# Linear attention feeding an RWKV channel mix: q transposed on TensorE instead of by DMA, units of 512/384/256 tokens with attention paced evenly, later loads on the GpSimd queue

## The chip, the cores and the metric

One core of one Trainium2 chip. The metric is device time in microseconds (us) of one execution, as a median of several. A ratio is the mean time of one kernel's fast runs over that of the other's in the same rounds, so it is not quite the ratio of the medians quoted beside it.

## The reference, cut to what matters

```python
# q, k, v: [8 batches, 8 heads, 576 tokens, 64], float32
q_s = softmax(q, over the 64 features);  k_s = softmax(k, over the 576 tokens)
kv  = einsum('bhsd,bhse->bhde', k_s, v)
x   = einsum('bhsd,bhde->bhse', q_s, kv)          # then heads side by side: [8, 576, 512]
xk, xr = x mixed with the token before it, by mu_k and by mu_r
k   = relu(xk @ w_k)                              # 512 -> 1024
out = sigmoid(xr @ w_r) * ((k * k) @ w_v)         # 1024 -> 512
```

## The kernel before

Attention runs in groups: 4 heads of one batch, 16 groups in all. A group loads q, k and v (0.59 MB each), takes exponentials on ScalarE, and TensorE forms `kv` (`kvp` in the code). To multiply the softmax of q by it, q must be transposed. The DMA engines do that:

```python
qt = apool.tile([128, J, 128], BF16, tag="qt", name="qt")
nc.sync.dma_start_transpose(out=qt[:], in_=qs[:].rearrange("p j c -> p (j c)"))
yield
for hf in range(2):
    ...                                    # cut: xp = kv^T q^T on TensorE, copied to xb by ScalarE
...                                        # cut: VectorE mixes xb with itself shifted: xd, xm, xk, xr
```

All loads, all transposes and all stores go through the SyncE queue, in that engine's order; the ten weight loads go through GpSimd's. TensorE's matmuls write to tiles of the pool `psum`, of which the channel mix has four (the PSUM buffers below). The channel mix works in 12 units of 384 tokens: 8 relu blocks of 4 matmuls into `kfp` (ScalarE takes the relu, VectorE squares it), then for each 128 tokens 4 matmuls into `rp` (ScalarE takes the tanh) and 8 into `vp` (VectorE multiplies and the result goes out). Both halves are generators and are interleaved:

```python
ASTEPS = 16            # an attention batch has 14 steps, so 16 a batch runs ahead of the units
MSTEPS = 14
for n in range(NU):                                            # NU = 12 units
    goal0 = done
    if n == 0:
        goal = ASTEPS
    else:
        goal = min((B - 1) * ASTEPS, ASTEPS + int(ASTEPS * n / 1.5) + 1)
    for i, _ in enumerate(unit(n)):
        want = goal0 + (goal - goal0) * (i + 1) // MSTEPS
        while done < want:
            next(att, None)
            done += 1
```

Below, "first unit" is the first piece of channel mix, and a "group" of batch 1 is "batch 1, group 0" or "group 1". A scheduler fixes each engine's order of instructions when the kernel is built. What stands behind a waiting instruction waits with it.

The softmax here doesn't subtract the row's maximum and nothing guards it: scores larger than these inputs give would overflow.

## Time and profile before

| | before |
|---|---|
| time, median (range) | 229.42 us (229.09 to 230.0) |
| span of the profiled run, TensorE clock granted | 228.1 us, 0.983 |
| busy: TensorE / VectorE / ScalarE | 182.5 / 160.1 / 136.0 us |
| first `vp` matmul; last matmul done | 50.3; 223.1 us |

The first `vp` matmul is a good milestone: the start is over by then, and nearly all the channel mix is still to come. The slices, stages and chain of this profile are shown in the prediction.

### The profile page before, as it was taken

Reading aid. Unit: us, or ns where it says so; the run is one execution under the profiler, and the core shown is the slowest. Engines: PE = TensorE matmul, PEld = TensorE weight load, DVE = VectorE, ACT = ScalarE, POOL = GpSimd, SP = SyncE. Lnnn points to the kernel's source line nnn. Section 1 sums busy time; section 2 is a strip of 40 time slices with the busy share of each in tenths; the row PEclk is TensorE's granted clock in tenths of the full one; section 3 lists DMA queues with packets and bytes.
Section 4 is the critical chain, followed back from the end, with each engine's and each line's share of the span. In section 5 each row is a group of like instructions: output and inputs, shape, how many; then the busy total and the mean of one; then the engine's idle time right before and its main releaser. Section 6 shows DMA issues by size and latency. Waiting matters only on the chain.

```text
span 228.1 us, 3352 instructions
## 1 busy us (share of the span) xinstructions
PE 182.5 (80%) x1153; PEld 92.8 (41%) x1169; DVE 160.1 (70%) x367; ACT 136.0 (60%) x213; POOL 7.1 (3%) x16
## 2 busy tenths in 40 slices
PE   0100055599989989979999999999999999999991
PEld 0100032254543534434544545545545454554540
DVE  0550077899989999799999999995867843343521
ACT  4544048699597886697685994946437254352720
POOL 2360000000000000000000000000000000000000
PEclk9999999599999999999999999999999999999999
DMA  6999999999799999999899899444041140414114
GB/s 222 362 318 207 195 314 393 259 334 285 171 303 295 247 318 232 279 293 275 282 264 313 248 277 275 92 93 98 3 92 46 40 101 1 111 26 95 46 46 95
DMA packets 40009, 45.32 MB, mean 199 GB/s; under 512 B 21048, under 2 KB 22584, under 8 KB 39992
## 3 DMA queue, kind: packets, MB, share of 16 engines
q1 hardware_dynamic: 37760, 42.48, 66.8%
q0 software_dynamic: 2208, 2.62, 6.7%
q8 instruction: 9, 0.15, 0.3%
q14 instruction: 8, 0.07, 0.1%
q10 hardware_dynamic: 24, 0.00, 0.0%
HBM read 33.56 MB, written 9.44 MB: 189 GB/s over the span
## 4 chain that ended last, share of the span: by engine, by line
PE 53%; DVE 18%; DMA 14%; SPq 7%; ACT 3%; issue 2%; DVEq 0%
PE vp L241 21%; PE kfp L223 19%; PE rp L234 10%; DMA raw<-in_q_dram 8%; SPq L189 5%; DMA raw<-in_k_dram 4%; DVE qs L169 3%; DVE rsum L165 3%; PE xp L194 2%; DVE xm L209 2%; DMA qt<-qs 2%; PE kvp L177 2%; DVE xd L203 2%; ACT eqk L157 2%; DVE xk L211 1%
## 5 line engine op out<-in xcount | busy, mean ns | idle before, releaser
L223 PE MATMUL kfp<-xk,wk_bf 128*128 128x384 bf16 x384 | 71.2, 336 | 7.0 <-DVE xk L211 6.4
L227 ACT ACTIVATE rel<-kfp 128x384 bf16<-128x384 f32 x96 | 45.9, 498 | 24.3 <-PE kfp L223 22.5
L223 PEld LDWEIGHTS <-wk_bf 128*128 128x128 bf16 x384 | 36.9, 100 | 34.8 <-issue 10.6
L157 ACT ACTIVATE eqk<-raw 128x1152 bf16<-128x1152 f32 x32 | 37.1, 1167 | 13.6 <-DMA raw<-in_k_dram 6.6
L244 DVE SCALAR_TENSOR_TENSOR ot<-th,vp 128x512 f32<-128x512 f32 x36 | 24.7, 685 | 23.9 <-PE vp L241 20.8
L237 ACT ACTIVATE th<-rp 128x512 f32<-128x512 f32 x36 | 21.6, 601 | 27.6 <-PE rp L234 27.1
L234 PE MATMUL rp<-wr_bf,xr 128*128 128x512 bf16 x132 | 36.5, 379 | 0.6
L194 PE MATMUL xp<-qt,w 128*128 128x512 bf16 x64 | 13.4, 306 | 18.3 <-DMA qt<-qs 17.0
L165 DVE TENSOR_REDUCE rsum<-eqk 128x18 f32<-128x1152 bf16 x16 | 21.4, 1339 | 6.8 <-ACT eqk L157 6.8
L169 DVE TENSOR_TENSOR qs<-eqk,rrec 128x1152 bf16<-128x1152 bf16 x16 | 21.7, 1354 | 0.2
L209 DVE TENSOR_SCALAR xm<-xd,mu 128x576 bf16<-128x576 bf16 x64 | 20.7, 367 | 0.1
L234 PEld LDWEIGHTS <-xr 128*128 128x128 bf16 x144 | 13.4, 98 | 14.2
L177 PEld LDWEIGHTS <-eqk 64*128 64x128 bf16 x288 | 9.4, 99 | 17.5 <-issue 9.7
L194 PEld LDWEIGHTS <-w 128*128 128x128 bf16 x64 | 5.8, 103 | 25.6 <-issue 15.5
L177 PE MATMUL kvp<-vv_100,eqk 64*128 64x129 bf16 x108 | 4.9, 232 | 10.4 <-ACT vv_100 L161 10.4
L197 ACT CAST xb_102<-xp 128x576 bf16<-128x576 f32 x12 | 7.6, 647 | 7.8 <-PE xp L194 7.8
L200 DVE COPY xb_102<-xb_102 128x126 bf16<-128x126 bf16 x6 | 1.2, 194 | 15.2 <-ACT xb_102 L197 15.2
L184 DVE SCALAR_TENSOR_TENSOR w<-kvp,rz,mask 128x128 bf16<-128x128 f32 x32 | 9.7, 342 | 0.2
L197 ACT CAST xb_110<-xp 128x576 bf16<-128x576 f32 x10 | 6.4, 639 | 4.6 <-PE xp L194 4.5
L161 ACT CAST vv_100<-raw 128x1152 bf16<-128x1152 f32 x6 | 7.0, 1167 | 1.5 <-DMA raw<-in_v_dram 1.5
L241 PE MATMUL vp<-wv_bf,k_961 128*128 128x512 bf16 x24 | 6.0, 380 | 1.7 <-DVE k_961 L229 1.7
L161 ACT CAST vv_108<-raw 128x1152 bf16<-128x1152 f32 x5 | 5.8, 1161 | 2.3 <-DMA raw<-in_v_dram 2.3
(75 smaller groups left out, 198.2 us busy)
## 6 DMA issues: line engine op xcount, KB each, us to landing
raw<-in_q_dram SPq DMA_DIRECT2D x16, 576.0 KB, 5.6
raw<-in_k_dram SPq DMA_DIRECT2D x16, 576.0 KB, 5.4
raw<-in_v_dram SPq DMA_DIRECT2D x16, 576.0 KB, 8.3
out_dram<-ot SPq DMA_DIRECT2D x72, 128.0 KB, 2.5
wk_bf<-in_moe_w_k_dram POOLq DMA_DIRECT2D x4, 256.0 KB, 7.6
wv_bf<-in_moe_w_v_dram POOLq DMA_DIRECT2D x2, 512.0 KB, 14.5
wr_bf<-in_moe_w_r_dram POOLq DMA_DIRECT2D x4, 128.0 KB, 11.1
qt<-qs SPq DMA_TRANSPOSE x16, 3.8
```

The lines of the kernel that those rows point to most:

```text
L157: nc.scalar.activation(out=eqk[:, i, :, :, :], in_=t[:, i, :, :].rearrange("p u (j d) -> p j u d", d=D), func=ACT.Exp)
L165: nc.vector.reduce_sum(out=rsum[:], in_=eq, axis=AX.X)
L169: nc.vector.tensor_tensor(out=qs[:].rearrange("p j (u d) -> p (j u) d", u=2), in0=eq, in1=rrec[:, :, None].to_broadcast((128, 2 * J, D)), ...
L177: nc.tensor.matmul(kvp[:, hf, 0:129], lhsT=eqk[r, 1, j, :, :].rearrange("p u d -> p (u d)"), rhs=vv[r, j, 0:129], start=(j == 0), stop=(j ...
L194: nc.tensor.matmul(xp[:, 64 * c:64 * e], lhsT=w[:, hf, :], rhs=qt[:, c:e, 64 * hf:64 * hf + 64], start=True, stop=True)
L209: nc.vector.tensor_scalar(out=xm[:, hf, :], in0=xd[:, hf, :], scalar1=mu[:, c:c + 1], scalar2=None, op0=ALU.mult)
L223: nc.tensor.matmul(kfp[:, 0:U], lhsT=wk_bf[:, ct, fc * 128:(fc + 1) * 128], rhs=xk[:, ct, c0:c0 + U], start=(ct == 0), stop=(ct == CT - 1))
L227: nc.scalar.activation(out=rel[:], in_=kfp[:, 0:U], func=ACT.Relu, scale=HALF_ROOT)
L234: nc.tensor.matmul(rp[:], lhsT=xr[:, ct, c0 + 128 * m:c0 + 128 * m + 128], rhs=wr_bf[:, ct, :], start=(ct == 0), stop=(ct == CT - 1))
L237: nc.scalar.activation(out=th[:], in_=rp[:], func=ACT.Tanh, scale=0.5)
L241: nc.tensor.matmul(vp[:], lhsT=k2[:, ft, 128 * m:128 * m + 128], rhs=wv_bf[:, ft, :], start=(ft == 0), stop=(ft == FT - 1))
L244: nc.vector.scalar_tensor_tensor(out=ot[:], in0=th[:], scalar=1.0, in1=vp[:], op0=ALU.add, op1=ALU.mult)
```

## The change

Its intent: take the transposes off the DMA engines and off the SyncE queue, start the first unit earlier, spread attention over the whole span, and let loads wait for nobody's results. The diff, cut to its core:

```diff
-    U = 384
+    UNITS = ((0, 512), (512, 384), (896, 256))
-    ldpool = ... bufs=4
+    ldpool = ... bufs=3
-    first = emit_load(0, 0)                      # all on nc.sync
-    emit_load(0, 1)
+    emit_load(0, 0, (nc.sync, nc.scalar, nc.sync))
+    first = emit_load(0, 1, (nc.scalar, nc.sync, nc.scalar))[0]
     ...                                          # weights: all gated on `first`, not only the first piece
-        nc.sync.dma_start_transpose(out=qt[:], in_=qs[:].rearrange("p j c -> p (j c)"))
+        qtp = psum.tile([128, 16, 128], BF16, tag="att", bufs=2, name="qtp")
+        for j in range(J):
+            nc.tensor.transpose(out=qtp[:, j, :], in_=qs[:, j, :], identity=ident[:])
+        nc.scalar.copy(out=qt[:], in_=qtp[:, 0:J, :])
     ...
-    emit_load(1, 0, wdone[3])
-    emit_load(1, 1, wdone[7])
+    emit_load(1, 0, (nc.gpsimd,) * 3)            # and so for all later batches
+    emit_load(1, 1, (nc.gpsimd,) * 3)
     ...
-    ASTEPS = 16
+    ASTEPS = 14
+    cols = 0
+    per_batch = S * (FT + CT * 3)
     for pair in range(B // 2):
         for c0, n in UNITS:
+            advance(ASTEPS * (2 * pair + (c0 + n - 1) // S))
+            for c in unit(pair, c0, n):          # unit() yields the columns it has spent
+                cols += c
+                advance(min((B - 1) * ASTEPS, ASTEPS * (cols + per_batch // 8) // per_batch))
```

More of the change, by code (lines that the diff above doesn't have):

```diff
@@ L46 @@
     FT = F // 128
-    U = 384
-    NU = B * S // U
-    assert B % 2 == 0 and (2 * S) % U == 0
+    UNITS = ((0, 512), (512, 384), (896, 256))
+    assert B % 2 == 0
     const = ctx.enter_context(tc.tile_pool(name="const", bufs=1))
-    ldpool = ctx.enter_context(tc.tile_pool(name="ldpool", bufs=4))
+    ldpool = ctx.enter_context(tc.tile_pool(name="ldpool", bufs=3))
     apool = ctx.enter_context(tc.tile_pool(name="apool", bufs=3))
@@ L66, in after, with emit_load @@
             tc.add_manual_dep(later.ins, earlier.ins.name, SYNC)
-    def emit_load(b: int, g: int, gate=None):
+    def emit_load(b: int, g: int, queues):
         t = ldpool.tile([128, 3, 2, J * D], F32, tag="raw", name="raw")
+        ld = []
         for i, src in enumerate((q, k, v)):
@@ L73, in emit_load @@
                          ap=[[J * D, 128], [2 * S * D, 2], [1, J * D]])
-            ld = nc.sync.dma_start(out=t[:, i, :, :], in_=ap)
-            after(ld, gate)
-            gate = None
+            ld.append(queues[i].dma_start(out=t[:, i, :, :], in_=ap))
         raw[b, g] = t
@@ L122, in emit_weights @@
                     after(done[-1], gate)
-                    gate = None
         for h in range(2):
@@ L130, in emit_weights @@
             done.append(nc.gpsimd.dma_start(out=wv_h, in_=ap))
+            after(done[-1], gate)
         return done
@@ L213, in attention, with unit @@
             yield
-    def unit(n: int):
-        xk, xr = xpair[n // 3]
-        c0 = U * (n % 3)
-        k2 = mpool.tile([128, FT, U], BF16, tag="k2", name="k2")
+    def unit(pair: int, c0: int, n: int):
+        xk, xr = xpair[pair]
+        k2 = mpool.tile([128, FT, 512], BF16, tag="k2", name="k2")
         for fc in range(FT):
@@ L222, in unit @@
             for ct in range(CT):
-                nc.tensor.matmul(kfp[:, 0:U], lhsT=wk_bf[:, ct, fc * 128:(fc + 1) * 128],
-                                 rhs=xk[:, ct, c0:c0 + U],
+                nc.tensor.matmul(kfp[:, 0:n], lhsT=wk_bf[:, ct, fc * 128:(fc + 1) * 128],
+                                 rhs=xk[:, ct, c0:c0 + n],
                                  start=(ct == 0), stop=(ct == CT - 1))
-            rel = mpool.tile([128, U], BF16, tag="rel", bufs=3, name="rel")
-            nc.scalar.activation(out=rel[:], in_=kfp[:, 0:U], func=ACT.Relu,
+            rel = mpool.tile([128, 512], BF16, tag="rel", bufs=3, name="rel")
+            nc.scalar.activation(out=rel[:, 0:n], in_=kfp[:, 0:n], func=ACT.Relu,
                                  scale=HALF_ROOT)
-            nc.vector.tensor_tensor(out=k2[:, fc, :], in0=rel[:], in1=rel[:], op=ALU.mult)
-            yield
-        for m in range(U // 128):
+            nc.vector.tensor_tensor(out=k2[:, fc, 0:n], in0=rel[:, 0:n], in1=rel[:, 0:n],
+                                    op=ALU.mult)
+            yield n
+        for m in range(n // 128):
             rp = psum.tile([128, C], F32, tag="mm", bufs=4, name="rp")
@@ L237, in unit @@
             nc.scalar.activation(out=th[:], in_=rp[:], func=ACT.Tanh, scale=0.5)
-            yield
+            yield 512
             vp = psum.tile([128, C], F32, tag="mm", bufs=4, name="vp")
@@ L246, in unit @@
             for i in range(2):
-                jb = (U * n + 128 * m) // 64 + i
+                jb = (2 * S * pair + c0 + 128 * m) // 64 + i
                 bb, j = jb // J, jb % J
@@ L251, in unit @@
                 nc.sync.dma_start(out=dst, in_=ot[64 * i:64 * i + 64, :])
-            yield
+            yield 1024
     def drain(gen):
@@ L256, in drain @@
             pass
-    wdone = emit_weights(first)
+    emit_weights(first)
     a0 = attention(0, 0)
@@ L273, in attention_of, with advance @@
                 if b + 1 < B:
-                    emit_load(b + 1, g, wdone[-1] if b == 1 and g == 0 else None)
+                    emit_load(b + 1, g, (nc.gpsimd,) * 3)
                 yield from attention(b, g)
-    ASTEPS = 16
-    MSTEPS = 14
+    ASTEPS = 14
     att = attention_of(range(1, B))
     done = 0
-    for n in range(NU):
-        goal0 = done
-        if n == 0:
-            goal = ASTEPS
-        else:
-            goal = min((B - 1) * ASTEPS, ASTEPS + int(ASTEPS * n / 1.5) + 1)
-        for i, _ in enumerate(unit(n)):
-            want = goal0 + (goal - goal0) * (i + 1) // MSTEPS
-            while done < want:
-                next(att, None)
-                done += 1
+    cols = 0
+    per_batch = S * (FT + CT * 3)
+    def advance(want):
+        nonlocal done
+        while done < want:
+            next(att, None)
+            done += 1
+    for pair in range(B // 2):
+        for c0, n in UNITS:
+            advance(ASTEPS * (2 * pair + (c0 + n - 1) // S))
+            for c in unit(pair, c0, n):
+                cols += c
+                advance(min((B - 1) * ASTEPS, ASTEPS * (cols + per_batch // 8) // per_batch))
     drain(att)
```

## The prediction

> **What bounds the kernel now.** I read the page's busy shares and slices first, then the stretches table cut at the chain's own joints, then the chain of waits itself. The slices:
>
> ```profile
> PE   0100055599989989979999999999999999999991
> DVE  0550077899989999799999999995867843343521
> PEclk9999999599999999999999999999999999999999
> DMA  6999999999799999999899899444041140414114
> ```
>
> One slice is 5.7 us. TensorE does almost nothing for seven slices, VectorE and the DMA engines are full until slice 24, and the last third is TensorE alone. The stretches table (columns: stretch and length, then busy us of PE, PEld, DVE, ACT and POOL with counts, granted clock, DMA share, GB/s) puts sizes on it:
>
> ```profile
> 0.00:42.33 42.33, 8.14 (x71) 4.84 (x72) 17.58 (x42) 19.58 (x19) 7.12 (x16) 0.97 1.04 287
> 42.33:125.15 82.82, 77.15 (x501) 37.97 (x509) 78.55 (x177) 63.14 (x98) 0.00 (x0) 0.98 0.99 277
> 125.15:184.11 58.96, 58.43 (x383) 30.24 (x386) 48.54 (x116) 36.09 (x64) 0.00 (x0) 1.00 0.51 127
> 184.11:223.10 38.99, 38.75 (x202) 19.76 (x202) 14.78 (x33) 17.19 (x33) 0.00 (x0) 1.00 0.27 62
> ```
>
> Four stages: a start of 42.3 us limited by transfers; 82.8 us in which DMA (0.99), VectorE (78.6 of 82.8) and TensorE are all nearly full and hinder one another; 59 us limited by TensorE with attention still in between; 39 us of pure channel mix (three units of 13.0 us, nothing beside them). The chain of waits, start and length in us:
>
> ```profile
> 15.26 9.87 SPq L189
> ...
> 26.88 9.15 DMA raw<-in_q_dram
> ...
> 42.33 4.00 PE kfp L223 x12
> ...
> 59.02 5.03 DMA qt<-qs
> ...
> 67.81 1.62 SPq L189
> 69.48 4.50 DMA raw<-in_k_dram
> ...
> 88.73 5.20 DMA raw<-in_k_dram
> ...
> 184.11 5.20 PE kfp L223 x32
> ...
> 223.11 0.69 DVE ot L244
> ```
>
> L189 is the DMA transpose of q. It holds the SyncE queue for 9.9 us in the start, the next loads queue behind it, and TensorE gets its first uninterrupted work at 42.33. Later the loads, which stand in the same queue behind outputs that wait for results, reach the chain three more times. From 184 on only TensorE is left, because attention was paced 16/14 too fast and had run out.
>
> **What the Trainium skill says.** "DMA: Bandwidth & Descriptors", section "Issuing engines are not separate DMA queues": DMAs started from different engines share the same 16 DMA engines and interleave; spreading them saves issue time only. The trace agrees as far as it goes: while the weights (GpSimd queue) and loads (SyncE queue) run together at the start, the DMA share is 1.04. So the new queues give no bandwidth; what they can give is freedom from waiting in line. "TensorE: Matmul & The Clock Gate", "Back-to-back issue gap": about 56 ns for an isolated 128-column matmul, about 81 ns sustained with a weight load for each. No 128-column transpose is in this trace; the nearest is the key-value product, 18 matmuls of 129 columns in half-height pairs in 0.63 us on the chain, so 70 ns a pair. The same page, "What's actually happening": the array starts at half clock until it has been busy about 3.4 us. The trace agrees: the first 12 matmuls of 384 columns at 42.33 took 4.00 us (333 ns each), later 32 of them 5.20 us (163 ns each). "SBUF — State Buffer", "SBUF: two separate sides": a GpSimd DMA's descriptors are written through a port that VectorE can hold shut. No run here shows it; before, GpSimd issued only the ten weight DMAs.
>
> **The change part by part.** (1) The 16 DMA transposes go. Their cost in DMA time is an estimate from this trace: the SyncE queue used 66.8% of 228.1 us, 152 us. Late in the kernel 18 outputs filled 26.3% of 39 us, 0.57 us each, so 72 outputs are 41 us. Back-to-back loads landed about 1.5 us apart (x 48 = 72 us). The rest, 39 us, is 2.4 us for each transpose. Need falls from 152 + 15 (weights, 6.7%) = 167 us, nearly all within the first 140 us, to about 128 us over the whole span: DMA stops being a bound after the start.
> (2) Added on TensorE: 9 transposes for each of 16 groups. At 56 to 81 ns, 0.5 to 0.73 us a group; I take 0.56, so 9.0 us in all, 7.8 us for the 14 groups after the start. All of it is on the path, since TensorE is the bound.
> (3) Added on ScalarE: 16 copies of 128x1152, about 1.17 us each by the row of the exponentials, 18.7 us. ScalarE goes from 136.0 to about 155 us. For two groups (one batch) its new load is 2 x (2.3 exp + 1.16 v + 1.17 q^T + 1.3 x) = 11.9, plus 6.0 for the relu and 2.7 for the tanh: 20.6 us.
> (4) Units of 512, 384, 256 instead of three of 384: the same columns, the same 96 relus (3 units a pair as before). Matmul time is per column, so nothing is gained there. The new sense is in when a unit may start: the first 512 tokens need one batch only, and attention is paced in step with the columns to the end. So the pure-TensorE last third disappears, and VectorE (about 20.2 us per batch: 7.0 per group for attention by its chain steps, and 6.2 for squares and outputs) and ScalarE (20.6) are loaded evenly beside TensorE, which needs 576/384 x 12.97 + 2 x (0.63 + 0.48 + 0.56) = 22.8 us per batch. All three are then at about 90% or more for most of the span.
> (5) Loads via GpSimd with three buffers. At 11.4 us a group and 4.5 us of transfer there is room. But batch 1's k and v now stand behind all weights in one queue.
>
> **The start in the new kernel**, by hand from rows of this trace. Six loads of batch 0 and q of batch 1: 7 x 1.5 us from 2.7 us, done about 13.5. ScalarE in its new order (three exps and copies for each group, then an exp of batch 1, then q^T copy 1.1, x copies 1.2, q^T copy, x copies, with half-clock matmuls between them): x of the second group about 25.0. VectorE then shift 0.2, difference 0.75, three scalings 0.85, sum 0.7: the first uninterrupted unit starts at about 27, not 42.3. The weights start when q of group 2 has landed (about 12) and take about 15 us, so k of batch 1 lands near 30 and v near 31.5. ScalarE's order has the exp of that k ahead of the first relu and the copy of that v ahead of the second. TensorE fills its four PSUM buffers and then waits, partly hidden by the half clock. Walking unit 0 through the engine orders, I get its end near 52 and unit 1's start near 54.5 (its second group's x mix comes after the fourth output on VectorE), where the sum of its matmuls would give 27 + 17.3 + 3.3 = 47.6. That is 6.5 to 7 us of stalls.
>
> **Sum.** Start 27.0. Channel mix 12 x 12.97 = 155.7. Attention of 14 groups at 1.67 = 23.4. From the last matmul to the end 5.1 as now (223.0 to 228.1), and 1.3 from span to time (229.42 against 228.1). Total 212.5 with no stall. Unit 0's stalls 6.5. Later stalls, where ScalarE has 10 us of work in a 512-column relu phase of 8.5 us of TensorE: I walk to 1 to 3 us per pair of batches and take 4 in all. Predicted: 223.0 us, 2.8% less than now. For comparison, the same no-stall sum for the kernel before, from 42.3 on, is 216.7 against a real 228.1; it lost 11 us to stalls, so 10.5 is not generous.
>
> **The rivals.** A: a full hand-over to ScalarE. The relus wait behind the exps and the new q^T copies, and TensorE stalls at every 512 unit and batch boundary. For it: 90% on three in-order engines and the order of relus and exps; my pessimistic walk gave up to 4 us per pair and 8 us in unit 0, so 228 to 231, no change. Against it: in the third stage now, with attention beside it, TensorE lost only about 1 us in 59; but ScalarE was at 61% there. B: TensorE stays full. The stalls of 42 to 125 us were the DMA's doing, as the three load pieces and the transpose in the chain suggest; then all but the start's stalls go: 215 to 218. C: loads come late, because GpSimd's descriptors are held up by VectorE or because three buffers are too few. For it: VectorE is busy nearly always. Against: each load has about 20 us of lead. It would make 230 to 240. D: transposes at 81 ns or above rather than 62: 2 to 3 us more.
>
> **Range and chances.** A and D upward and B downward are of like weight, C is small: 215 to 231 for 8 in 10. The 2% line is 224.8, close above my figure, so faster 0.57, same 0.37, slower 0.06.
>
> **What would show it.** Right: first full relu-phase matmuls at 25 to 29 us; a DMA share well under 0.9 after 40 us; no load in the chain after 45 us; q^T transposes at 55 to 80 ns each and nine in line; ScalarE at about 155 us; TensorE full to the last slice with attention in it. Wrong: TensorE's waits for relus or for x mixes summing to over 12 us after 55 us (rival A), exps waiting for GpSimd loads after 45 us (rival C), or a first unit that starts after 32 us (my start is wrong).

## The result, and the profile after

| | before | after |
|---|---|---|
| time, median (range) | 229.42 us (229.09 to 230.0) | 223.86 us (223.1 to 224.28) |
| ratio, 95% interval | | 0.9751 (0.9717 to 0.9786) |
| span, clock granted | 228.1, 0.983 | 221.9, 0.999 |
| busy: TensorE / VectorE / ScalarE | 182.5 / 160.1 / 136.0 | 191.7 / 166.2 / 147.7 |
| first `vp` matmul; last matmul done | 50.3; 223.1 | 39.8; 216.8 |

2.5% faster, 0.9 us above the predicted time. The slices of the changed kernel (one is 5.5 us):

```profile
PE   0045748999999999999999999999999999999990
DVE  1539758999999898889798998888777757482431
DMA  6979999999999274789075290242131401330413
```

TensorE starts two to three slices earlier and is full to the end; the DMA engines are no longer full after slice 12. The stretches, cut at the same times as before (same columns):

```profile
0.00:42.33 42.33, 20.38 (x142) 10.92 (x142) 26.11 (x62) 24.90 (x31) 15.73 (x28) 1.00 0.97 287
42.33:125.15 82.82, 80.69 (x574) 43.20 (x573) 75.60 (x160) 67.97 (x106) 19.77 (x28) 1.00 0.72 258
125.15:184.11 58.96, 58.19 (x405) 30.26 (x404) 47.30 (x108) 40.86 (x67) 1.83 (x3) 1.00 0.30 80
184.11:221.90 37.79, 32.43 (x196) 17.15 (x194) 17.21 (x40) 13.96 (x27) 0.00 (x0) 0.99 0.27 63
```

TensorE did 20.4 us of work in the first 42 us instead of 8.1. The DMA share of the second stretch fell from 0.99 to 0.72. ScalarE's work there rose from 63.1 to 68.0 us. The chain of waits:

```profile
14.45 5.93 DMA wk_bf<-in_moe_w_k_dram
20.66 10.20 DMA raw<-in_k_dram
30.88 1.16 ACT eqk L155
32.04 0.49 ACT rel L227
...
47.43 1.02 ACT qt L190
48.49 0.41 PE xp L195 x2
...
89.28 0.67 DVE xk L212
...
95.44 1.11 ACT qt L190
...
208.00 3.49 PE kfp L223 x32
...
216.77 0.69 DVE ot L245
```

The last load on the chain ends at 30.9: it is k of batch 1, which stood behind the weights in GpSimd's queue. From there on no transfer is on it. In place of the loads stand ScalarE's new copy of the transposed q (L190), its relus, and VectorE's token mix. The timeline of the start (start, length, engine, line, instruction, and in brackets the idle time before it and what ended it) shows what the load did:

```profile
29.55 1.89 PE L223 MATMUL kfp<-xk,wk_bf 128*128 128x512 bf16 x8 [1.91 <-DVE xk L212]
30.88 1.16 ACT L155 ACTIVATE eqk<-raw 128x1152 bf16<-128x1152 f32 x1 [4.03 <-DMA raw<-in_k_dram]
31.95 0.58 ACT L227 ACTIVATE rel<-kfp 128x512 bf16<-128x512 f32 x1
32.58 0.59 PE L223 MATMUL kfp<-xk,wk_bf 128*128 128x512 bf16 x2 [1.14 <-ACT rel L227]
```

ScalarE waits 4.0 us for k of batch 1. The first relu stands behind that exponential in its order, and TensorE, with its four PSUM buffers full, waits for the relu.

**An account in three terms.** The span splits into the time to the first `vp` matmul, the TensorE work from there to the last matmul, and the stalls in between. The work is a sum: weight loads counted after the milestone (they are complete in the trace, where some matmul records are missing), times the spacing the chain shows for a full pipeline: 0.217 us for 512 columns (8 in 1.73), 0.1625 for 384 (32 in 5.20), 0.109 for 256 (32 in 3.49), 0.63 us for the `kvp` of a group, 0.24 for each half of `xp`, 0.50 for nine transposes. Before: 352 relu matmuls x 0.1625 + 428 others x 0.217 + 12 x 0.63 + 26 x 0.24 = 163.8. After: 55.6 for the 352 relu matmuls (96 of 512, 128 of 384, 128 of 256) + 92.9 + 13 x 0.63 + 6.2 + 13 x 0.50 = 169.3 (totals are good to 0.1). Stalls are what is left over.

| us | first `vp` | TensorE work after it | stalls | last matmul |
|---|---|---|---|---|
| before | 50.3 | 163.8 | 9.0 | 223.1 |
| after | 39.8 | 169.3 | 7.7 | 216.8 |

The start gave 10.5 us. The work took back 5.5 of them: 6.5 of transposes, 0.6 of one group's `kvp` that moved behind the milestone, less 1.6 because a first unit of 512 tokens has more of its relu matmuls ahead of it. The stalls hardly moved. This table is carried through all the experiments. Each row comes from one profiled run, and the runs of one kernel differ by more than 1 us (before: 228.3 to 231.1 over all rounds), so differences of stalls below about 1.5 us are not read.

### The profile page after: what moved, and what is told of

The parts are those of the page before. It is cut to its first block, busy times and chain, and to the rows that moved or that the text cites.

```text
span 221.9 us, 3634 instructions
## 1 busy us (share of the span) xinstructions
PE 191.7 (86%) x1313; PEld 101.5 (46%) x1313; DVE 166.2 (75%) x367; ACT 147.7 (67%) x229; POOL 37.3 (17%) x58
## 3 DMA queue, kind: packets, MB, share of 16 engines
q0 software_dynamic: 8256, 27.40, 38.4%
q1 hardware_dynamic: 6576, 11.21, 17.2%
## 4 chain that ended last, share of the span: by engine, by line
PE 57%; DVE 15%; DMA 12%; ACT 10%; issue 2%; ACTq 1%; POOL 1%; DVEq 0%
PE vp L242 23%; PE kfp L223 15%; PE rp L235 11%; DMA raw<-in_q_dram 5%; DMA raw<-in_k_dram 5%; PE xp L195 3%; ACT rel L227 3%; ACT eqk L155 3%; ACT qt L190 3%; DMA wk_bf<-in_moe_w_k_dram 3%; PE kvp L175 3%; DVE rsum L163 2%; DVE xk L212 2%; DVE xm L210 2%; PE qtp L189 2%
## 5 line engine op out<-in xcount | busy, mean ns | idle before, releaser
L223 PE MATMUL kfp<-xk,wk_bf 128*128 128x384 bf16 (+2 forms) x384 | 71.1, 329 | 4.0 <-DVE xk L212 2.3
L227 ACT ACTIVATE rel<-kfp 128x512 bf16<-128x512 f32 (+2 forms) x96 | 45.8, 517 | 20.7 <-PE kfp L223 19.4
L223 PEld LDWEIGHTS <-wk_bf 128*128 128x128 bf16 x384 | 35.8, 98 | 28.8 <-issue 6.8
L238 ACT ACTIVATE th<-rp 128x512 f32<-128x512 f32 x36 | 22.9, 635 | 21.9 <-PE rp L235 20.9
L74 POOL DMA_DIRECT2D raw<-in_q_dram x14 | 10.2, 731 | 73.2 <-ACT vv_108 L159 31.8
L190 ACT COPY qt<-qtp 128x1152 bf16<-128x1152 bf16 x16 | 18.2, 1137 | 4.3 <-PE qtp L189 4.1
L235 PEld LDWEIGHTS <-xr 128*128 128x128 bf16 x144 | 13.2, 98 | 13.9
L189 PE MATMUL qtp<-ident,qs 128*128 128x128 bf16 x144 | 11.6, 231 | 0.0
L189 PEld LDWEIGHTS <-qs 128*128 128x128 bf16 x144 | 9.9, 103 | 2.6 <-issue 0.4
L74 POOL DMA_DIRECT2D raw<-in_v_dram x14 | 10.1, 723 | 2.3 <-DMA wv_bf<-in_moe_w_v_dram 1.8
L74 POOL DMA_DIRECT2D raw<-in_k_dram x14 | 10.1, 721 | 2.3 <-DMA wv_bf<-in_moe_w_v_dram 1.4
## 6 DMA issues: line engine op xcount, KB each, us to landing
out_dram<-ot SPq DMA_DIRECT2D x72, 128.0 KB, 2.4
```

The source lines that it names most:

```text
L74: ld.append(queues[i].dma_start(out=t[:, i, :, :], in_=ap))
L189: nc.tensor.transpose(out=qtp[:, j, :], in_=qs[:, j, :], identity=ident[:])
L190: nc.scalar.copy(out=qt[:], in_=qtp[:, 0:J, :])
L223: nc.tensor.matmul(kfp[:, 0:n], lhsT=wk_bf[:, ct, fc * 128:(fc + 1) * 128], rhs=xk[:, ct, c0:c0 + n], start=(ct == 0), stop=(ct == CT - 1))
L227: nc.scalar.activation(out=rel[:, 0:n], in_=kfp[:, 0:n], func=ACT.Relu, scale=HALF_ROOT)
L235: nc.tensor.matmul(rp[:], lhsT=xr[:, ct, c0 + 128 * m:c0 + 128 * m + 128], rhs=wr_bf[:, ct, :], start=(ct == 0), stop=(ct == CT - 1))
```

## The experiments

Each kernel was correct. "Theory 1" in the expectations is: the DMA transposes cost the start and DMA time; TensorE is the bound after it and pays for the new transposes in full; the rest is small. Rival A: ScalarE hands over to TensorE and binds as much. Rival C: the loads are tight.

### One part alone: PE transposes in the kernel before

```diff
 # kernel before
-        nc.sync.dma_start_transpose(...)
+        (the nine PE transposes and ScalarE's copy)
```

> The kernel before with one part of the change alone: q is transposed by TensorE and copied out by ScalarE; old units, old pacing, old queues. Theory 1 (the DMA transposes cost the start and the DMA time, and TensorE pays about 8 us for their removal): the first uninterrupted relu-phase matmul starts 8 to 14 us earlier than 42.3, the DMA share between 42 and 125 falls from 0.99 to about 0.75, and the time is 222 to 227 us. Rival (the gain comes from units, pacing and queues, and the transposes alone only add work to TensorE and ScalarE): 231 to 238 us.

226.90 us, ratio to before 0.9894 (0.9838 to 0.9951): just inside theory 1's range. The first uninterrupted relu matmuls start at 32.5, 9.8 us earlier, as expected. The first `vp` came at 43.7 instead of 50.3, the DMA share between 42 and 125 was 0.84 (0.75 expected). Account: 43.7 + 170.3 + 6.2 = 220.2. So 6.6 us from the start, 2.8 from stalls, less 6.5 of transposes.

### One part alone: units and pacing in the kernel before

```diff
 # kernel before
-    U = 384
+    UNITS = ((0, 512), (512, 384), (896, 256))
     # and the new unit() and pacing loop; DMA transposes and SyncE loads stay
```

> The kernel before with the units of 512, 384, 256 and the even pacing alone; DMA transposes and SyncE loads stay. Theory 1 (columns cost what they cost, and the start and the DMA transposes set the rest): the start stays above 40 us, loads and transposes are spread more evenly so the DMA share between 42 and 125 falls somewhat below 0.99, and the time is within 3 us of the kernel before, 227 to 232 us. Rival (pacing is worth something by itself): 225 us or less.

225.14 us, ratio 0.9812 (0.9758 to 0.9867). Theory 1 is missed, and the rival all but met: this part alone brings 4.3 us of the 5.6 that the whole change brings. The stretch from 42 to 125 us of this kernel:

```profile
42.33:125.15 82.82, 81.42 (x516) 41.19 (x522) 76.87 (x164) 60.39 (x97) 0.00 (x0) 0.97 1.01 286
```

The DMA engines are still full (1.01; before 0.99), the start is still late (first `vp` at 50.9), and yet TensorE is busy for 81.4 us there instead of 77.2. Account: 50.9 + 162.8 + 4.5 = 218.2, so the stalls fall from 9.0 to 4.5. Full DMA engines as such did not stall TensorE. The likely reading is demand: with pacing 16/14 too fast, attention asked for 16/14 of the loads, exponentials and VectorE work per unit, more than those engines could give; with even pacing they just keep up. The two traces fit it. Between 50 and 125 us the kernel before starts 9 groups of attention, this one 8; VectorE is busy for 71.8 and 70.5 of the 75 us; ScalarE's exponentials wait 3.8 us for loads before, and for none here. Of the 5.2 us of waits that the trace lists for TensorE there before, 4.0 end with a result of VectorE and 0.7 with a DMA transfer. What is not shown is which half of the edit does it: unit sizes and pacing were changed together, here and in the run that undoes them, and a first unit of 512 tokens also leaves more time before batch 1 is needed.

### One part undone: DMA transposes back in the changed kernel

```diff
 # changed kernel
-        (the nine PE transposes and ScalarE's copy)
+        nc.sync.dma_start_transpose(out=qt[:], in_=qs[:].rearrange("p j c -> p (j c)"))
```

> The changed kernel with the DMA transposes put back on the SyncE queue; units, pacing and GpSimd loads stay. Theory 1: TensorE loses 8 us of transposes, but transposes wait in the start behind transfers and the DMA share rises again to over 0.9 until about 140 us, so 226 to 232 us. Rival (TensorE is the only bound after the start, DMA is hidden now that loads have their own queue): 8 us less than the changed kernel, 214 to 218 us.

237.51 us, ratio to before 1.0330 (1.0255 to 1.0404): slower than the kernel before, beyond theory 1's range and far from the rival's. Its chain:

```profile
17.79 12.81 DMA qt<-qs
...
50.30 16.36 DMA qt<-qs
```

Two transposes, 12.8 and 16.4 us from issue to landing (the median of the seven whose landing this trace shows is 6.4), stand on the chain while loads on their own queue keep the DMA engines full. TensorE waits 13.9 us for the second of them, most of the stalls below, and its clock is granted at about half in the two slices from 59 to 71 us. Account: 46.5 + 162.8 + 22.1 = 231.4. So units plus GpSimd loads need the PE transposes; the gains of the parts don't add up, they depend on one another. That the free-running loads are what stretches these two transposes is the likely reading; no run here separates it from the order of the queue. A transpose as slow as this also stands in the start of the kernel before (16.5 us, 10.1 of them on SyncE itself) and of the units-and-pacing run (16.4), whose loads go through SyncE; new here is the slow one at 50 us, after the start.

### One part undone: old units and pacing in the changed kernel

```diff
 # changed kernel: units of 384, ASTEPS = 16 and the old loop
```

> The changed kernel with units of 384 and the old pacing (16 steps a batch, so attention runs out early); PE transposes and GpSimd loads stay. Theory 1 (matmul time goes by columns and TensorE is full anyway): ScalarE and VectorE are pressed harder in the first 125 us and idle in the last third, 1 to 4 us more than the changed kernel, 224 to 228 us. Rival (even pacing is the main gain): 229 us or more.

224.88 us, ratio 0.9783 (0.9739 to 0.9827), against 0.9751 for the whole change: inside the range, and the intervals overlap, so up to about 1 us. Account: 38.6 + 170.9 + 7.8 = 217.3, the same stalls as the changed kernel. Once the transposes are off the DMA engines, the units and pacing that were worth 4.5 us of stalls alone are worth almost nothing. That both cures treat the same shortage is the reading that fits; it was not tested otherwise.

### One part undone: loads on SyncE in the changed kernel

```diff
 # changed kernel
-    emit_load(..., (nc.gpsimd,) * 3)
+    emit_load(..., (nc.sync,) * 3)
```

> The changed kernel with the loads of batches 1 to 7 issued from SyncE instead of GpSimd; all else stays. Theory 1 (a queue gives no bandwidth, only freedom from waiting in line): batch 1 lands before the weights are done, so the stall in the first unit shrinks by some 3 to 5 us, while the weights land later; afterwards loads stand behind outputs and some exponentials wait for them, 2 to 4 us; in sum 221 to 226 us. Rival C (loads are tight, three buffers and one queue decide): 228 us or more, with waits for loads over 8 us after 55 us.

226.92 us, ratio 0.9878 (0.9842 to 0.9915), just past theory 1's range and short of rival C's. The chain has q of batch 2's group 1 landing at 39.1 and a store with 7.6 us at 48.5. The loads did come early, but they slowed the weights: the two pieces of `w_v` land at 39.2 and 44.9 instead of 26.8 and 29.4. First `vp` at 42.7, stalls about 9. The queue of its own is worth some 3 us.

### Twice the transposes

```diff
         for j in range(J):
-            nc.tensor.transpose(...)
+            for _ in range(2):
+                nc.tensor.transpose(...)
```

> The changed kernel with every PE transpose done twice (the second overwrites the first with the same values). Theory 1 (TensorE is the bound for nearly all of the time after the start, and nine transposes take 0.50 us warm): 14 groups after the start x 0.50 = 7 us, and about 1 us in the start, so 230 to 232.5 us. Rival A (ScalarE and VectorE hand over, TensorE has slack): under 227 us.

231.87 us (231.78 to 232.14): 8.0 us more, theory 1. Sixteen groups x 0.50 = 8.0. The milestone moved by 2.1 us and the rest by 6.3 (13 groups x 0.50 = 6.5). The added transposes are paid in full.

### Twice ScalarE's copy

```diff
-        nc.scalar.copy(out=qt[:], in_=qtp[:, 0:J, :])
+        for _ in range(2):
+            nc.scalar.copy(out=qt[:], in_=qtp[:, 0:J, :])
```

> The changed kernel with ScalarE's copy of the transposed q done twice, 1.1 us more for each of 16 groups, 18 us more work on ScalarE (148 to 166 us busy). Theory 1 (ScalarE has slack in the rp and vp phases, but sits on the chain in the relu phase of the 512 units and in the start): 3 to 9 us more, 227 to 233 us. Rival A (ScalarE binds as much as TensorE): 12 us or more on top, 236 us or more. If ScalarE has real slack: under 226 us.

230.11 us (20 runs): 6.25 us more, in the middle of theory 1's range. About 18.2 us of added ScalarE work (16 x 1.14) cost 6.25: 3.3 in the start (first `vp` at 43.1) and 3.6 after it in the profiled run. ScalarE is not the bound but has little slack: one third of what is added to it comes out in the time.

### The copy on VectorE

```diff
-        nc.scalar.copy(out=qt[:], in_=qtp[:, 0:J, :])
+        nc.vector.tensor_copy(out=qt[:], in_=qtp[:, 0:J, :])
```

> The changed kernel with the transposed q copied out by VectorE instead of ScalarE. Theory 1 (after the start TensorE is the bound, and both helpers are at about 90% of its pace): VectorE comes to about 22.5 us per batch against 22.7 for TensorE, so some 2 to 6 us slower, 226 to 230 us. Rival A (ScalarE is what hands over to TensorE): 222 us or less.

226.51 us (9 runs), ratio 0.9884 (0.9850 to 0.9918): in theory 1's range, but for another reason than it gave. VectorE's copy takes 0.74 us, not 1.1. All the loss is in the start: the first `vp` came at 44.6, 4.8 us later, because VectorE's order put the second group's copy behind the first group's token mix, and the TensorE clock dropped to half for two slices there. From the milestone to the end it took 176.2 us against 177.0. So after the start no difference shows between the two engines' copies.

### Four load buffers

```diff
-    ldpool = ... bufs=3
+    ldpool = ... bufs=4
```

> The changed kernel with four load buffers instead of three; the order of instructions on every engine is the same, only the loads may start earlier. Theory 1 (loads have a lead of about 20 us after the start): no change, 223 to 225 us. Rival C (three buffers are too few): 221 us or less.

223.86 us, ratio 0.9751 (0.9698 to 0.9804): no change, with the order of instructions identical on every engine. So three buffers are not too few. The other half of rival C, loads held up when GpSimd issues them, shows nowhere either: in the changed kernel ScalarE waits for no load after 45 us.

### The start, first try: batch 1's first group ahead of w_r and w_v

```diff
-    emit_weights(first)
+    emit_weights(first, between=load of batch 1, group 0, gated on `first`)   # after w_k
```

> The changed kernel with the start mended: the first group of batch 1 is loaded from the GpSimd queue after w_k and before w_r and w_v, and q of it no longer beside batch 0. Theory 1 (in the first unit TensorE stalls because ScalarE's exponential and copy for k and v of batch 1, which land behind all weights, stand ahead of the first relus): k lands near 24 instead of 31 us, batch 0 lands 1 to 1.5 us earlier, and 4 to 7 us go: 217 to 220 us. Rival (the start is set by ScalarE's chain and the half clock, not by the landing): 222 us or more.

224.02 us: a miss. The load did land early, but the scheduler had built another order on ScalarE:

```profile
21.79 1.16 ACT L158 ACTIVATE eqk<-raw 128x1152 bf16<-128x1152 f32 x1 [3.94 <-DMA raw<-in_q_dram]
23.30 1.16 ACT L158 ACTIVATE eqk<-raw 128x1152 bf16<-128x1152 f32 x1 [0.35 <-DMA raw<-in_k_dram]
24.37 1.10 ACT L193 COPY qt<-qtp 128x1152 bf16<-128x1152 bf16 x1
```

The exponential of batch 1's q now stands ahead of batch 0's last copy of the transposed q and waits 3.9 us for its load. The stall for k was traded for one for q, at an even worse place; the first `vp` is at 40.4.

### The start, second try: batch 0 on one queue in the order of need

```diff
 # added to the first try
-    emit_load(0, 0, (nc.sync, nc.scalar, nc.sync))
-    first = emit_load(0, 1, (nc.scalar, nc.sync, nc.scalar))[0]
+    emit_load(0, 0, (nc.sync,) * 3)
+    first = emit_load(0, 1, (nc.sync,) * 3)[0]
```

> As the run that loaded the first group of batch 1 before w_r and w_v, and besides all six loads of batch 0 on one queue in the order of need. In that run k of batch 1 landed at 23.3 instead of 30.9 us, but ScalarE's order had changed: the exponential of q of batch 1 stood ahead of the second group's q^T copy and waited 3.9 us for its landing, so nothing was gained. Here that exponential stands between the two x copies of the second group. Theory 1 (the landing matters, through whatever ScalarE has in line behind it): the first group of batch 0 is done earlier, at most 1 us of waiting is left, 217 to 221 us. Rival (the start is set by ScalarE's own work and the half clock): 222 us or more.

220.71 us, ratio 0.9644 (0.9606 to 0.9682): in the range. Three queues had shared the bandwidth among loads needed at different times: in the changed kernel k of batch 0's first group is waited for until 11.49 us (q's exponential had ended at 7.4). In line, they arrive when they are needed. First `vp` at 36.8.

### The start, third try: ScalarE's order forced

```diff
 # added to the second try: in attention(), for (b, g) == (1, 0)
+            after(ex, lastx[0])        # exponentials of batch 1 only after batch 0's last x copy
```

> As the run before it in this call, and the exponentials of batch 1's first group are forced to stand after the last x copy of batch 0 on ScalarE. Theory 1: the first uninterrupted relu-phase matmul at 25 to 27.5 us (29.6 in the changed kernel), no relu waits behind a load, the first unit ends at 47 to 49 us instead of 52.5, and the time is 217 to 219.5 us. Rival: 222 us or more.

218.73 us (218.26 to 219.36), ratio to before 0.9555 (0.9519 to 0.9591): the fastest kernel here, ahead of both. The answer to the start shown above:

```profile
22.31 2.22 ACT L159 ACTIVATE eqk<-raw 128x1152 bf16<-128x1152 f32 x2
24.43 1.14 ACT L165 CAST vv<-raw 128x1152 bf16<-128x1152 f32 x1
24.98 2.29 PE L229 MATMUL kfp<-xk,wk_bf 128*128 128x512 bf16 x5 [2.95 <-DVE xk L218]
26.03 0.60 ACT L233 ACTIVATE rel<-kfp 128x512 bf16<-128x512 f32 x1 [0.46 <-PE kfp L229]
```

Batch 1's exponentials and v copy are done before the first relu is due, and that relu waits for its matmul instead of the matmul for it. First `vp` at 34.2, so 5.6 us earlier than in the changed kernel; the time fell by 5.1. The rest of the span is 1.4 us longer in the profiled run, which was the slowest of the four: 34.2 + 169.3 + 9.1 = 212.6.

All in one table, from the profiled runs (stalls are rounded differences):

| us | time | first `vp` | TensorE work after | stalls |
|---|---|---|---|---|
| before | 229.4 | 50.3 | 163.8 | 9.0 |
| only PE transposes | 226.9 | 43.7 | 170.3 | 6.2 |
| only units and pacing | 225.1 | 50.9 | 162.8 | 4.5 |
| all but PE transposes | 237.5 | 46.5 | 162.8 | 22.1 |
| all but units and pacing | 224.9 | 38.6 | 170.9 | 7.8 |
| the change | 223.9 | 39.8 | 169.3 | 7.7 |
| the change, start mended | 218.7 | 34.2 | 169.3 | 9.1 |

## Why the prediction was right or wrong

The time (223.86 for 223.0) and most steps held; the reason given for one gain did not.

- **Start.** Predicted 27 for the first uninterrupted unit, measured 29.55, just outside the 25 to 29 set as its test. The term that was short is ScalarE's line: the last x copy of batch 0 was put at about 25.0 and ends at 26.85, after a wait of 4.1 us for batch 0's k (until 11.49) early in that line. (Besides, 25.0 and the prediction's own 2.5 on VectorE make 27.5, not 27.) The doubled-copy and mended-start runs confirm that this line sets the start: the milestone moves with it.
- **Unit 0.** The stall was foretold in kind and place: k of batch 1 behind all weights (foretold near 30, waited for until 30.88), the first relu behind its exponential. The uninterrupted start of unit 1 was put at 54.5 and is at 54.76, but that closeness is partly luck: two errors cancel. By the prediction's own sum, 29.55 + 17.3 + 3.3 = 50.15, so the stalls up to there were 4.6, not 6.5 to 7, and the start was 2.5 late. The three tries at the start, ending 5.1 us faster, show that the late start and this stall together could be recovered; they don't part the two.
- **Transposes.** 0.56 us per group predicted, 0.50 measured, paid in full (8.0 us more when doubled). The 56 ns that the Trainium skill ("TensorE: Matmul & The Clock Gate", "Back-to-back issue gap") gives for an isolated matmul held: the chain has 0.50 us for nine.
- **DMA.** The need was put at about 128 us. Measured: the queues' shares, 17.2%, 38.4% and 2.1% of 221.9 us, make 128.0. The estimate of 2.4 us of DMA time for a transpose was right.
- **ScalarE.** 155 us busy predicted, 147.7 measured. The copies cost what was said (18.2 us for 16, against 18.7). The busy figure counts overlapping neighbours once: summing the groups' own times gives about 167 us after and 145 before, so the step "136 + 18.7" mixed a union with a sum.
- **Stalls after the start.** Predicted 2.5 at the boundary of unit 0 and 1, and 4 later. From the last matmul of unit 0 (about 52.2) to the end the span is 164.6 us; the work there is 10 units' worth of channel mix, 4096 tokens x 12.97/384 = 138.3, and 12 groups x 1.61 = 19.3, so 7.0 us of stalls against 6.5. The size was right. In the prediction's own terms the late start (+2.5) and the smaller stalls in unit 0 (-1.9) nearly cancel, the later stalls are 4.4 for 4 (counted as the prediction counts, with no work of unit 1 before 54.76), and 14 groups of transposes are 0.9 cheaper. So the total is nearer than its terms.
- **What the stalls were made of before** was wrong. The prediction's rival B, and its step (1) with it, put the stalls between 42 and 125 us on the DMA engines ("the DMA's doing"), and step (4) said of units and pacing that in matmul time "nothing is gained there". The units-and-pacing run has the DMA engines just as full and half the stalls: full DMA engines were not enough to stall TensorE. What the traces show in their place is waits mostly for VectorE (4.0 of 5.2 us) while attention ran ahead of the units. So demand is the likely cause, but unit sizes and pacing were not run apart. Removing DMA load and removing the excess demand look like two cures for one shortage, and the second is the cheaper: it costs TensorE nothing.
- **Readings.** Two in the prediction are loose. TensorE did almost nothing for five slices, not seven (the sixth to eighth read 5). After 42 us two loads and one transpose stand on the chain shown, not three loads.
- **The rivals.** A was half true: ScalarE gives back a third of what is put on it, though after the start no difference shows whether it or VectorE copies. B failed as an outcome: the stalls stayed at 7.7 where B needed about 1; what fills the place of the DMA waits is not shown. C fell with the four-buffer run and with ScalarE waiting for no load after 45 us. D fell with 0.50 us.

What the change lacked was in part visible before it ran (the late k of batch 1 was foretold): it gave 10.5 us in the start and left 5 more there. What stays open: why the stalls after the milestone are 6.2 to 9.1 with PE transposes and 4.5 with even pacing and DMA transposes. The copies on ScalarE are one part (3.6 us when doubled), but the copy on VectorE left the rest of the span unchanged, so they can't be all of it. Whether PE transposes for batch 0 alone, with DMA transposes later, would keep both the early start and the small stalls was not run; the slow run with DMA transposes beside GpSimd loads is a warning.

## What to carry to other kernels

When three engines are all near full, don't read the fullest one as the cause: look at how fast the other half of the program is being asked to run, and try pacing it to what is consumed first; here units and pacing alone gave 4.3 us of the 5.6. In the start, put transfers in one line in the order of need, and check in which place of an in-order engine the first instruction that waits for each transfer stands; moving a transfer also moves that instruction. Split a span into start, work and stalls before and after: work moved onto the bounding engine was paid there in full here, and was worth it only for what it freed in the other two terms.

## What the Trainium skill lacked or had wrong

- "TensorE: Matmul & The Clock Gate", "Back-to-back issue gap": gives about 81 ns at 128 columns and about 131 ns at 512 as sustained spacing with a weight load each. Here nine transposes of 128 columns with a weight load each took 0.50 us (56 ns), and 512-column matmuls with a weight load each went at 217 ns (8 in 1.73 us). The page's isolated formula fits both, its sustained figures neither.
- The same page, "Part 4: PE-mode transpose": about 275 ns for a transpose in context. The records here have a median of 219 ns each, but back to back they cost 56 ns; for a run of transposes the spacing is what counts.
- "SBUF — State Buffer", "SBUF: two separate sides", has VectorE starving GpSimd's descriptor writes. Not seen here: with VectorE busy 75.6 of 82.8 us, issuing a load from GpSimd took 709 to 838 ns throughout, and such loads landed in as little as 4.3 us. Whether any VectorE instruction here is of the kind that the page means was not tested.
- "DMA: Bandwidth & Descriptors", "DMA Transpose (X-bar)": the section says nothing of how long a transpose takes beside other traffic. From issue to landing the median is 3.8 us in the kernel before, but up to 16.5 us with loads in flight.
